# One list of the order of all instructions replaced by another: attention read and gated MLP on one core

## The chip, the cores and the metric

The kernel runs on one core of a Trainium2 chip. The metric is the device time of one execution in microseconds (us), the median of a few runs. TensorE is called PE in the profile, its weight loads PEld, VectorE DVE, ScalarE ACT, and SP is the SyncE queue from which this kernel issues all of its DMAs.

## What is computed

```
# x: B=8, H=8, S=512, D=64      state: B=8, H=8, Ns=32, D=64
scores  = scale * x @ state^T              # 512 x 32 for each (b, h)
xread   = softmax(scores)  @ state
scores2 = scale * state @ x^T              # 32 x 512
sread   = softmax(scores2) @ x
t = concat([xread, sread], axis=2)         # 8 x 8 x 544 x 64
t = t.transpose(0, 2, 1, 3).reshape(-1, 512)   # the reference reshapes these 4352 rows ...
out = ((t @ w_a) * (t @ w_b)) @ w_out      # d_model 512, d_ff 1536
```

The result is fp32. Nearly all of the work is the gated MLP: three products of some 4,350 tokens with matrices of 512 x 1536.

## The kernel before, in words

Every fp32 operand of a large product is split into a high and a low part (`_h`, `_l`), and a product is three matmuls: high by high, high by low, low by high. The names in the profile are tiles: `x_raw` and `stg` hold inputs as loaded, `wo` is a pool of 512-wide tiles that serve as scratch (loaded states, weights in the making, identity matrices), `raw` and `p_raw` hold fp32 values on their way to a split, `p_h`, `p_l` are split weights, `at_h`, `at_l` split tokens, `ab` is the PSUM of layer 1, `a_sb` its product, `g_h`, `g_l` the split gate result, `acc` the PSUM of layer 2 and `ms` the PSUM of everything small. `out<-stg` stores the result.

Tokens are taken batch by batch, d_ff in chunks; the attention of a batch comes ahead of its tokens, and the state reads (`raw<-e_dram`, `sd_h<-xn`, then the PE group `ms<-raw,sd_h`) are made in four places, the first of them about half way.

What sets the order: the code does not issue its instructions as it goes. A `Recorder` notes each operation as a unit with a running number, 0 to 4595 (2699 units on PE, 837 on DVE, 695 on ACT, 365 DMAs on SP). A unit is one to a few dozen instructions on one engine. A text `ORDER` (lines 137 to 323) lists all unit numbers, `arranged` reads it, and the end of `attn_moe` issues the units in that order:

```python
    with tc.manual_schedule():
        for i in arranged(rec.units):
            for obj, method, args, kw in rec.units[i].calls:
                getattr(obj, method)(*map(real, args), **{k: real(x) for k, x in kw.items()})
```

So every instruction has line L1105 in the profile, and each engine and the SP queue work through their own units in the order of the list. Waits between engines follow from the tiles. A DMA on SP waits until its tile is free, until its data are there, and for the eighth DMA ahead of it to have landed, since eight semaphores are used in turn; whatever stands behind it on SP waits with it.

Units that are spoken of below, with what they do:

| units | engine | what |
|---|---|---|
| 34; 107 | PE | `ms<-x_raw`, 8 matmuls; the second for the next input |
| 62, 68 | SP | loads `raw<-w_out` |
| 106 | SP | second load of `x_raw` |
| 204, 208; 997, 994 | SP | loads `wo<-wl`; `wo<-sd` (512 KB each) |
| 137, 138; 295, 296, 576 | SP | loads `wo<-xt` of states, 64 KB each |
| 18, 59, 60 | ACT, ACT, PE | a split `p_l`; `at_h<-ab`; the PE matmul that needs `at_h` |
| 61, 66, 80 | ACT, ACT, PE | `at_l<-ab`; `wo<-t`; the PE matmul that needs `at_l` |
| 205, 108, 109 | ACT, ACT, PE | `t<-wo`; `x_nat<-ms`; the transposes that need `x_nat` |
| 139, 160 | PE | `ms<-p_raw,wo`, 32 matmuls, which needs 137 and 138; then the first `acc<-wo,g_h` |
| 2649, 2651, 2653, 2656, 2667 | SP | last five loads for the first state read, 64 KB and (2667) 512 KB |
| 2668 | PE | the group `ms<-raw,sd_h` that needs them |
| 4467, 4471, 4475; 4513 | ACT | copies `stg<-acc`; a copy `a_sb<-ab` |
| 4511 | PE | the matmul `ab<-x_raw,wq`, 256 wide |

Of the kernel before, what the change touches and what calls it, by code (L numbers as in the profile page):

```python
# [142 lines left out]
73 144 120 135 192 105 136 150 145-146 209-210 200 214 201 151 2672 226 211 152-154 528 213 196 147 218 148 362 149  # L143
215 188 529 156 189 530 155 193 217 190 157 197 191 172 366 173 219 174-175 222 176 221 194 177 158 178 223 370 198
232 184 228 195 535 531 179 233 253 202 235 180 234 181 199 237 256 236 238 203 182-183 227 259-260 185 532 254 374
239 229 240-242 536 159 262 363 263 297 533 224 186 225 534 230 243 294 244 364 249 257-258 365 378 255 298 264 231
284 367 245 281 537 368 265 290 187 291 384 246-247 369 541 248 285 803 266 250 267 540 268 372 542 282 251 269 577
271 371 270 252 272 261 300 373 1004 273 287 277 288 299 274 375 275 289 301 998 283 324 376 325 302 538 276 1002
303-304 377 539 305-306 278 292 379 327 307 380 279 390 996 1022 318 386 391 319-320 393 308 392 309 314 310-311 394
312 346 381 347 286 321 280 322 385 313 543 382 387 315 388 330 767 326 546 354 1031 331 544 332 1013 348 355 383 518  # L150
349 356 333-334 357 1006 335-336 316 547 337-338 342 317 339-341 545 560 395 549 396-397 548 323 350 1005 328 343 398
351 550 329 344 358-359 562 352 551 399 353 401 804 563 402 768 400 552 360 411 553 361 414 417 403 407 404 554-555
405 1007 406 412 423 564 424-425 561 426 1008 565 415 408 420-421 413 556 1009 416 442 451 557 389 558 429 452 430 422
1014 448 453 431 427 454 428 1015 418 568 345 419 443 409 439 455 440 432 1000 445 1016 446 433-434 1017 435 578 410
# [993 lines left out]
```

## Time and profile before

| | |
|---|---|
| median of 3 runs | 669.38 us (669.19 to 669.46) |
| profiled execution | 669.68 us, of which the span of the trace is 667.8 us |
| granted TensorE clock in it | 1.0 of full speed |
| PE busy | 655.6 us (98% of the span) |
| PEld, DVE, ACT busy | 521.8, 438.1, 384.3 us |
| DMA queue | 122.71 MB, 55.4% of 16 engines |

The span is counted from the first instruction to the last; the 1.9 us between it and the execution's time lie around it. Each run is one execution on one core.

### The profile page before, as it was taken

To read this page: it belongs to the slowest core of one execution; us is meant where nothing else is said; L and a number is where in the kernel's file an instruction comes from. 1 tells how busy PE (TensorE), PEld (TensorE's weight loads), DVE (VectorE), ACT (ScalarE), POOL (GpSimd) and SP (SyncE) were. 2 spreads that over 40 slices of the span, in tenths; PEclk is the share of its full clock that TensorE was granted. 3 is DMA by queue.
4 is the path that set the end of the run, shared out by engine and by line. 5 is a ranking of instruction groups with operands and counts; after the bars stand their busy time and mean duration, and the time that the engine had idled before them with its cause. 6 is when DMAs were issued, how large, how long until landed. Compare 5 with 4: busy or idle time off the path is not lost.

```text
span 667.8 us, 10023 instructions
## 1 busy us (share of the span) xinstructions
PE 655.6 (98%) x3676; PEld 521.8 (78%) x3676; DVE 438.1 (66%) x837; ACT 384.3 (58%) x712; POOL 0.7 (0%) x6
## 2 busy tenths in 40 slices
PE   5999999999999999999999999999999999999997
PEld 1677777778888887887887887888888888888886
DVE  5889988875645567867667475846857545565433
ACT  4887763779986776866534343535556444454333
POOL 0000000000000000000000000000000000000000
PEclk9999999999999999999999999999999999999999
DMA  8878422296899759865865558756067230512002
GB/s 319 280 230 268 145 65 92 95 353 228 288 310 316 249 165 315 271 222 183 275 210 152 196 163 250 246 186 226 27 206 240 75 127 0 190 31 79 1 0 111
DMA packets 59776, 123.34 MB, mean 185 GB/s; under 512 B 9936, under 2 KB 18384, under 8 KB 59728
## 3 DMA queue, kind: packets, MB, share of 16 engines
q1 hardware_dynamic: 59728, 122.71, 55.4%
q8 instruction: 29, 0.48, 0.3%
q14 instruction: 19, 0.16, 0.1%
HBM read 85.46 MB, written 37.22 MB: 184 GB/s over the span
## 4 chain that ended last, share of the span: by engine, by line
PE 95%; DMA 3%; DVE 0%; issue 0%; SPq 0%; ACT 0%; ACTq 0%
PE ab L1105 44%; PE acc L1105 42%; PE ms L1105 9%; DMA wo<-xt 1%; DMA raw<-w_out 1%; DMA raw<-wl 1%; DVE p_raw L1105 0%; SPq L1105 0%; DVE t L1105 0%; ACT t L1105 0%; DVE stg L1105 0%; ACT a_sb L1105 0%; DVE m L1105 0%; ACTq L1105 0%
## 5 line engine op out<-in xcount | busy, mean ns | idle before, releaser
L1105 PE MATMUL acc<-wo,g_h 128*128 128x512 f32 (+1 forms) x824 | 268.9, 389 | 0.0
L1105 PEld LDWEIGHTS acc<-wo,g_h 128*128 128x128 f32 x824 | 153.7, 188 | 33.0 <-issue 1.7
L1105 PE MATMUL acc<-wo,g_l 128*128 128x512 f32 x412 | 153.9, 389 | 0.0
L1105 PE MATMUL ab<-at_l,p_h 128*128 128x512 f32 x384 | 148.8, 391 | 0.0
L1105 PE MATMUL ab<-at_h,p_h 128*128 128x512 f32 x384 | 147.0, 394 | 0.0
L1105 PE MATMUL ab<-at_h,p_l 128*128 128x512 f32 x384 | 146.9, 391 | 0.0
L1105 DVE TENSOR_TENSOR a_sb<-ab,a_sb 128x512 f32<-128x512 f32 (+1 forms) x108 | 71.2, 659 | 113.2 <-PE ab L1105 68.5
L1105 ACT COPY a_sb<-ab 128x512 f32<-128x512 f32 x120 | 67.9, 567 | 112.4 <-PE ab L1105 96.9
L1105 ACT CAST g_h<-a_sb 128x512 fp32r<-128x512 f32 (+1 forms) x108 | 64.2, 598 | 54.4 <-DVE a_sb L1105 34.5
L1105 DVE TENSOR_TENSOR g_l<-a_sb,g_h 128x512 fp32r<-128x512 f32 (+1 forms) x108 | 70.8, 657 | 32.5 <-ACT g_h L1105 25.1
L1105 PEld LDWEIGHTS acc<-wo,g_l 128*128 128x128 f32 x412 | 77.3, 188 | 16.5 <-issue 0.8
L1105 PEld LDWEIGHTS ab<-at_h,p_h 128*128 128x128 f32 x384 | 71.9, 188 | 22.8 <-issue 2.1
L1105 PEld LDWEIGHTS ab<-at_h,p_l 128*128 128x128 f32 x384 | 72.1, 188 | 17.6 <-issue 2.5
L1105 PEld LDWEIGHTS ab<-at_l,p_h 128*128 128x128 f32 x384 | 72.1, 188 | 15.6 <-issue 0.8
L1105 DVE TENSOR_TENSOR p_l<-p_raw,p_h 128x512 fp32r<-128x512 f32 x72 | 48.6, 683 | 15.0 <-ACT p_h L1105 14.8
L1105 ACT CAST p_h<-p_raw 128x512 fp32r<-128x512 f32 x72 | 43.2, 621 | 14.8 <-PE ab L1105 13.5
L1105 DVE SCALAR_TENSOR_TENSOR t<-t,t 128x512 int32<-128x512 int32 x60 | 41.1, 685 | 10.4 <-ACT t L1105 9.3
L1105 ACT ACTIVATE t<-raw 128x512 f32<-128x512 f32 x42 | 28.3, 674 | 5.4 <-issue 1.0
L1105 ACT CAST wq<-raw 64x512 fp32r<-64x512 f32 x40 | 24.6, 618 | 9.8 <-DVE raw L1105 8.3
L1105 PE MATMUL ms<-wq,sd_h 128*128 128x512 f32 x72 | 28.0, 390 | 0.0
L1105 PE MATMUL ms<-wq,sd_l 128*128 128x512 f32 x72 | 28.0, 389 | 0.0
L1105 ACT COPY sw_st<-ms 128x512 f32<-128x512 f32 x40 | 22.5, 586 | 7.0 <-PE ms L1105 6.0
(131 smaller groups left out, 600.4 us busy)
## 6 DMA issues: line engine op xcount, KB each, us to landing
p_raw<-scr SPq DMA_DIRECT2D x36, 512.0 KB, 5.1
raw<-wl SPq DMA_DIRECT2D x34, 512.0 KB, 6.0
scr<-sw_st SPq DMA_DIRECT2D x40, 256.0 KB, 5.6
out<-stg SPq DMA_DIRECT2D x33, 256.0 KB, 4.9
scr<-wo SPq DMA_DIRECT2D x32, 256.0 KB, 3.3
wo<-wl SPq DMA_DIRECT2D x10, 512.0 KB, 7.2
x_raw<-xt SPq DMA_DIRECT2D x8, 576.0 KB, 6.0
raw<-w_out SPq DMA_DIRECT2D x8, 512.0 KB, 4.8
```

The lines of the kernel that those rows point to most:

```text
L1105: getattr(obj, method)(*map(real, args), **{k: real(x) for k, x in kw.items()})
```

## The change

Only the text `ORDER` is replaced. The new list holds the same numbers, so the kernel issues the same instructions on the same engines, in another order on each engine and on SP. Its beginning, the place of the first state read and its end, as lines of the diff:

```diff
 ORDER = """
-5 1 6 10-11 19 23 121-122 34 994 3 35 2 520 36 137 4 8 7 37 576 0 48 62 9 38 68 20-21 521 39 22 25 49 40 24 50 522 26
-12 51 27 13 41 52 16-17 106 42 123 53 43 295 28 204 54 31 63 44 997 64 14 208 32 55 45 56 296 57 15 46 18 138 525 47
-58 65 74 59 75 29 70 76 69 293 523 77 60 30 107 71 61 524 66 212 526 80 216 67 108 78-79 124 81 206 109 86 125 33 110
-90 72 91 126 92 995 82-83 111 84-85 127 93 112 94-95 87 128 139 113 88 129 160 140 96 114 130 97 115 142 131 98 116
-163 102 166 169 141 527 167 99 143 100 164 205 117 132 101 118 170 220 89 161 133 103 119 134 168 162 207 104 165 171
...
-2584 2110 2116 2650 2127 2112 2128 2667 2117 2165 2651 2129 2054 2130 2748 2131 2121 2656 2143 2755 2133 2586 2120
...
-2761 2187-2188 2177-2178 2762 2226 2179 2196 2763 2668 2181 2749 2158 2750 3186 2154 2189 2677 2202 2680 2197 2674
...
-4469 4539 4467 4477 4470 4506 4475 4507-4508 4471 4509-4510 4519 4513 4511 4522 4478 4515 4525 4540-4541 4516
...
+0 5 34-35 1 6 10-11 19 23 3 2 520 36 62 4 121 521 8 7 122 37 68 9 48 38 20 39 21-22 204 25 49 40 24 50 522 26 12 51 41
+27 13 52 16 14 123 106 42 53 43 137 295 997 31 54 44 17 55 32 64 63 45 994 56 28 15 57 46 525 47 58 65 74 18 75 59 76
+523 69 60 70 77 66 29 71 107 138 61 205 208 80 108 212 216 524 293 576 81 78 540 124 79 109 67 206 526 207 220 86 125
+110 30 82 33 296 83 126 111 127 84 90-91 85 92-93 112 94-95 87 128 139 113 88 72 114 129 160 163 166 96-99 167 140 115
...
+2049-2051 2118-2119 2138 2755 2740 2744-2746 2140 2649 2656 2653 2667 2651 1935 1866 3184 2113 2116 2168 2155 2117
+2143 2578 2169 2167 2747 2120 2147 2156 2148-2149 2748 2144-2146 2756 2170 2174 2171 2760 2122 2175 2668 3166 2749
...
+4449-4452 4445-4446 4453-4454 4447-4448 4457 4459 4472-4474 4455-4456 4496 4475 4458 4497-4501 4460-4463 4502-4506
+4512 4469 4507-4511 4513 4515 4519-4520 4540-4541 4470-4471 4539 4542-4544 4548-4552 4514 4516-4518 4545-4546 4522
```

## Rows read from the trace of the kernel before

**Rows 1.** The profile's page: busy time by engine, and the chain that ended last.

```profile
PE 655.6 (98%) x3676; PEld 521.8 (78%) x3676; DVE 438.1 (66%) x837; ACT 384.3 (58%) x712; POOL 0.7 (0%) x6
...
PE 95%; DMA 3%; DVE 0%; issue 0%; SPq 0%; ACT 0%; ACTq 0%
```

**Rows 2.** Windows: length, then busy PE, PEld, DVE, ACT, POOL; clock, DMA share, GB/s.

```profile
0.00:10.00 10.00, 3.02 (x12) 0.92 (x12) 2.73 (x6) 3.43 (x5) 0.70 (x6) 1.00 0.78 272
10.00:20.00 10.00, 8.41 (x65) 3.55 (x65) 8.89 (x20) 6.94 (x17) 0.00 (x0) 1.00 0.98 353
20.00:30.00 10.00, 9.78 (x72) 6.14 (x72) 8.65 (x20) 8.98 (x18) 0.00 (x0) 1.00 0.97 341
30.00:90.00 60.00, 60.00 (x348) 44.51 (x347) 55.31 (x103) 44.99 (x83) 0.00 (x0) 1.00 0.59 190
90.00:640.00 550.00, 550.00 (x3056) 446.36 (x3055) 352.18 (x669) 311.52 (x574) 0.00 (x0) 1.00 0.55 183
640.00:668.00 28.00, 24.35 (x129) 20.34 (x127) 10.30 (x23) 8.46 (x18) 0.00 (x0) 1.00 0.18 66
```

**Rows 3.** The chain that ended last, 0 to 30 us: start, length, what.

```profile
10.52 7.08 DMA raw<-w_out
...
19.43 8.41 DMA wo<-xt
```

**Rows 4.** Timeline of PE, 0 to 35 us and 58 to 110 us.

```profile
4.41 1.94 PE L1105 MATMUL ms<-x_raw 128*32 128x512 f32 x8 [4.41 <-DMA x_raw<-xt]
...
21.37 1.07 PE L1105 MATMUL ms<-x_raw 128*32 128x512 f32 x8
...
26.68 1.07 PE L1105 MATMUL ms<-p_raw,wo 64*32 64x256 f32 x16
27.97 1.07 PE L1105 MATMUL ms<-p_raw,wo 64*32 64x256 f32 x16 [0.22 <-DMA wo<-xt]
28.97 0.50 PE L1105 MATMUL acc<-wo,g_h 128*128 128x512 f32 x1
...
80.67 1.20 PE L1105 MATMUL ms<-p_raw,wo 64*32 64x256 f32 x32
```

**Rows 5.** Timeline of the SP queue, 0 to 24 us: start and length of the issue.

```profile
16.12 0.33 SPq L1105 DMA_DIRECT2D x_raw<-xt  x1
...
18.74 2.25 SPq L1105 DMA_DIRECT2D wo<-xt  x2
```

**Rows 6.** DMA issues, 0 to 30 us: count, KB each, median us to landing.

```profile
wo<-xt SPq DMA_DIRECT2D x5, 64.0 KB, 7.6
```

**Rows 7.** Timeline of ACT, 16 to 33 us.

```profile
18.79 0.66 ACT L1105 CAST p_l<-acc 128x256 fp32r<-128x256 f32 x2
...
19.96 0.59 ACT L1105 CAST at_h<-ab 128x512 fp32r<-128x512 f32 x1
...
30.77 0.68 ACT L1105 ACTIVATE t<-wo 128x512 f32<-128x512 f32 x1
```

**Rows 8.** Timeline of the end, all engines, 653 to 668 us.

```profile
653.42 1.57 ACT L1105 COPY stg<-acc 128x512 f32<-128x512 f32 x3 [0.99 <-PE acc L1105]
...
654.86 0.39 PE L1105 MATMUL acc<-wo,g_h 128*128 128x512 f32 x1
655.06 0.37 ACT L1105 COPY a_sb<-ab 128x256 f32<-128x256 f32 x1
...
655.48 0.39 PE L1105 MATMUL ab<-x_raw,wq 128*128 128x256 f32 x1 [0.23 <-ACT a_sb L1105]
...
661.51 0.30 PEld L1105 LDWEIGHTS acc<-wo,g_l 128*128 128x128 f32 x2 [0.16 <-DVE g_l L1105]
```

**Rows 9.** First state read: SP timeline, PE timeline, DMA issues 330 to 348 us.

```profile
336.33 1.46 SPq L1105 DMA_DIRECT2D raw<-e_dram  x2
...
347.29 0.65 PE L1105 MATMUL ms<-sd_h,raw 128*32 128x64 f32 x32
...
raw<-e_dram SPq DMA_DIRECT2D x7, 64.0 KB, 5.3
```

More of the change, by code (lines that the diff above doesn't have):

```diff
@@ new lines @@
+901 1252 1204 942 946-949 927 1215 928 1193-1194 1216 1205 924 1207 1206 920 1253-1254 925 1327 1208 943 926 929 1225
+1195-1196 1221 923 954 931 950 932 963 1222 951 1249 1237 964-965 952 991 1250 1209 870 1320 1210 960 955-956 1319
+1218 982 966 1226 972 1321 961 1255 973 1239 1217 1223 1322 1101 644 1219 1211 1103 1102 967-968 1212 969-971
+1323-1324 1220 1104 974-975 1325 992 962 1227 957 1228 976-977 958 978 1224 1328 1238 993 959 979 1229 1326 980 1240
+1336 1256 953 988-989 1230 1105 1329 1111-1112 1241 1330 990 1231 1331 1257 1113-1116 1233 981 1232 1106-1108 1234
@@ new lines @@
+1109-1110 983-984 1332-1334 985 1335 986 1127 1354 987 1356 1130 1345 1117 871 1128-1129 1242 1355 1357 1118 1155 1124
+1370 1337 1358 1371 1131 1133 1359 1235 1134-1135 1119 1372 1360 1243 1338-1342 1125 1156 1120 1126 1139 1347
+1140-1141 1152 1236 1132 1142 1158-1159 1361 1343-1344 1402 1244 1153 1346 1373 1364 1160 1136-1138 1287 1258 1475
+1348 1362 1260 1145 1143 1259 1363 1349-1351 1261 2679 1374 1144 1262 1157 1284 1121 1378 1146 1263 1379 1365 1375
+1264 1288 1122 1394 1285 1352 1268 1123 1353 1380 1289 1381 1265-1267 1366 1269 1367 1270-1271 1368 1376 1272 1369
@@ new lines @@
+1286 1154 1149-1150 1274 1147-1148 1377 1281-1282 1403 1395 1273 1408 1290 1382 1275 1404 1151 1276-1277 1384 1405
+1383 1283 1309 1312 1291 1385 1315 1292 1278 1414 1293 1316 1294 1477 1295 1386 1390 1296-1298 1397 1299 1302 1387
+1398 1391 1300 1313 2285 1314 1441 1409 2060 1301 1406 1396 1310 1392 1279-1280 1306-1308 1435 1303-1304 1415
+1410-1411 1305 1311 1438-1440 1442-1443 1436 1417 1478 1416 1418 1317 1546 1479 1407 2294 1388 1466 1419-1422 1467
+1668 1444-1445 1400 2287 1423-1425 1431 1426-1428 1480 1429-1430 2286 1447-1449 1437 1468 1432 1450-1452 1459 1412
@@ new lines @@
+1446 2288-2289 1453-1456 2290-2291 2720 1481 1463 1457 1464 1469 1607 1389 1458 1393 1465 1482 1433 1460 1401
+1483-1484 1399 1434 1470 1461 1488-1489 1485 2292 1462 1498 1486 1472-1474 1507 1487 2293 1413 2295 2303 2296 2712
+2321 1494 2297 1501 2323 1490-1491 2298 1471 2299-2300 1510-1513 1547 1492-1493 1495 1499 1504-1506 1500 1514 1496
+2301-2302 2312 1497 1548 1476 1515 1534-1535 1508-1509 1516-1521 1608 1526-1527 1502-1503 1536 1530-1532 1522 2322
+2324 1549 2304 1538 1523 1539 1551 2305 1528 1552 2325 1550 1557 1553-1554 2306 1672 1529 1537 1567-1568 1533 1669
@@ new lines @@
+1609 1555 1558 1610 1540 2307 1556 1541 2327 1559 1563 1560 1570 2308 1561-1562 1579-1580 1564 1524 1573 2309 1576
+1571 1581 2326 2313 1582 2314 1574 2328 1583 2315 1585-1586 2310 1587 2316 1577 2337-2338 2340 2339 1569 1611 1525
+2317 1572 1595 1584 2318 1588 2311 1589 2331 1591 2406 1590 2329 1544 1741 2319 1592 1596 2330 1612-1615 1578
+1604-1605 2320 1616 1618 1565 1673-1674 2415 2341 1566 1617 1624 1675 1598-1600 1631 1597 1619 2407 1628 2333-2334
+1575 1620-1623 1640 1625 2408 2332 1593 2342 2409 1641 2410 2669 1594 1629 1642 1632-1633 1643 1601 1644-1645 2061
@@ new lines @@
+1602-1603 1634 2411-2413 1652 1659 1626 2062 2417 1646-1648 2414 2063 1676 1606 1637-1638 1649-1651 2416 2424 2080
+2733 2067 1627 1653 1802 1677-1679 2343 2418 1680 1635-1636 1662 2064 1681-1682 2419 1639 1683-1684 2420-2421 1665
+1654 2422 1630 2065 2423 1656-1657 1660 2078-2079 2335 2068 1689 1658 1685-1686 2336 2081 2069 1687-1688 2083 2344
+1663 1661 1666-1667 1702-1703 1690 2433 2426 1864 2066 2442 2082 1705 1693 2070 1696 1711-1715 2673 1742 2425 2427
+1706-1709 2428 2071 1691 1542 2444 1664 1699-1701 1655 2086 1744 2443 2458 1692 1697 2445 1710 1717 1545 1694 1704
@@ new lines @@
+2446 1803 2447 1733 1746 2429-2430 1698 1725 2435 1743 1695 2431 1734-1736 1716 1726 2448 2432 1727-1728 2449 2527
+1747 1721 2434 2461 2450 1729-1731 1718 1748 1543 1722-1723 2436 1745 2072 1740 2459 1752-1753 1724 1754-1755
+1749-1751 2452 1805 1758 1719 1756 1762 2437 1732 1757 1763 2438-2439 1804 1759 1739 1863 2529 2073-2074 2440 2460
+1867 1774-1778 2528 2441 1806 2530 1764 1720 2536 1780-1781 1779 1786 1765 1768 1771-1773 1769-1770 1766 1796
+1782-1784 1790-1792 1785 2531-2533 2075 1799-1800 1807-1811 1760-1761 2451 2453 2463 2462 1812 1819 1787 1767 1793
@@ new lines @@
+1788 1794 1789 1823 1813 2534 1824 1814-1815 2535 1816 2545 1835-1836 1817-1818 1936 1820 2734 1868 1870 1837
+2454-2455 1838 1869 2537 1797 1839 1841-1844 1840 2538 1847 2539 2456 2076 1845-1846 1795 1826 2457 1872 1871 2077
+1873 1997 1798 1801 1832-1833 1829 2464 1848 1878-1879 1830 1827-1828 1831 1821 1874-1877 1822 2084 2540-2543 1849
+2544 1884 1880-1882 1670 1937 1939 1671 2085 2465 1737 2554 1834 2546 1860 2721 1938 1940 2547 1825 2087 2565 1854
+1851 1855 2563-2564 2548 1852 2566 2579 1900 1861 1901 1883 1885 1902 1856 1891-1892 1862 1897 1903-1904 1893 1905
@@ new lines @@
+2094 2580 2732 2088 1850 1912 2089-2091 1898-1899 2567-2568 2581 1928 2549 2670 1906 1857-1859 1894-1896 1924 1920
+1853 1888-1889 1941 1907 2718 1942 1886-1887 1921 1908 2550 1909 1890 1916-1918 1910-1911 1929 1922 1943 1913
+1944-1945 2551 1946 1914 1925 1953 1930 2556 1919 2569 1915 1926-1927 1923 1947 2652 1969-1973 1998 1738 1948-1950
+2552 1957 1999 2570 1951-1952 2000 2555 2557-2558 1954 2559 1960 2735 2560-2561 1958 2736 1934 1974 1981 2562
+1975-1976 2553 2648 2658 2657 1963-1964 1977 1959 1978-1979 1931 2752-2753 2092 1961-1962 1988 1955 1980 1966 2737
@@ new lines @@
+1982 1967 1983 1965 2001 2741 2738 2665 2163 2650 1968 1994 2664 2002 1991 2003 1865 2008 2004 1985-1987 1995 2009
+2005 2010 2006 1989 2582 2666 2007 1932 2661 2011-2013 2571 1956 2014-2015 2030-2033 1996 1990 2021 2739 2036 2572
+2095 2097 2027-2028 2037-2039 2034 2040 2093 2029 2654 2055 2583 1984 2096 2098 2224 2659 2041 2056 2035 2042
+1992-1993 2024-2026 2018-2019 2573 2164 2016 3169 2022 2099 2574 2100 2742 2101 2057 2124 2020 2102 2754 2043 2575
+2584 2103 2576 2104 2663 2743 2105-2106 2660 2125 2585 2577 2655 2107 2044 2108 2662 2046-2048 2115 2052 2109-2110
@@ new lines @@
+2345 2690 2181-2182 2197-2200 2190-2192 2201 2694 2700 2697 2202-2204 2212 2208 2158 2758 2213 2205-2206 2228 2162
+2759 2207 2193-2195 2229 2214 2685 2209 2183 2217 2709 2696 2692 2218 2245 2701 2586 2707 2693 2230 2683 2686 2684
+2346-2347 2688-2689 2231 2235 2246-2247 2236 2210 2232 2219-2220 2233-2234 2221 2241 2222 2237-2240 2242-2243 2223
+2257 2254 2251 2255 2211 2263-2264 2252 2258-2261 2265-2268 2248-2249 2262 2269-2271 2466 3187 2348 2706 2703 2691
+2695 2705 2349 2587 3221 2708 2698 2764 2256 3188-3190 2282 3193 2283 2273-2275 2284 2366-2367 2253 2279 2244 2702
@@ new lines @@
+2250 2276-2278 2369 2350 2280 2351 2281 3191 2352 2765-2767 3194 2467 2272 2356-2359 2372-2374 2360-2361 2353-2355
+2362-2364 2469 2365 3206 2468 2375 3192 3207 2376-2377 2368 2394 2378-2379 2395 3208 2403-2405 2380-2384 2396
+2385-2389 2710 2390-2391 2470-2477 2483 3195 3151 3256 2370-2371 2397 2392 2719 3161 2713 2768 3257 2588 2716 2722
+2590 3204-3205 3209 3196 2398 2589 2591 2399 2478-2482 2484 2490 2499-2500 2496-2498 2524 2723 3142 3152 2393
+2400-2402 2485-2486 2505 2731 2729 2501 3143 2506-2507 3220 3154 2837 2502-2503 2491 2504 2511 2508 3212 2509
@@ new lines @@
+2493-2494 2510 2592-2593 3163 2487-2489 2515 3277 2512 3213 2726 3197-3200 2160 3157 2730 3214-3215 3164 2513 2769
+2728 2725 3172 2770 2594-2597 2604 2771 2727 3201 3222 3202 2525 2772 2516 3158 3160 3145 2492 2526 2518-2520 3173
+3203 2724 2611-2613 2617-2618 2495 3210 2898 3211 3144 3261 2598-2601 2620 2602-2603 2517 2608 2514 2605 2521-2523
+2614 2621 2609 2615-2616 2642-2643 2622 2626-2629 2623-2624 2610 2630 2625 2631 2639 2606 3159 3156 3155 3264 3150
+3280 2644 2632-2633 2607 2636 2634 2838-2839 2637 2773-2774 2619 3149 2161 2779-2780 3146 3263 2781-2784 2775-2778
@@ new lines @@
+2785 3170 2786 3223 3216 2801 2645 2795 2646 2640 2647 2798 2807 2641 2808-2811 3148 3265 3217 3153 3147 2796 2638
+2789-2791 2802-2806 2635 2813 3218 2812 2799-2800 3224 3278 3226 2814 2829 2817 2842-2843 2818-2819 2792 2899 2840
+2820 2841 2959 2830-2831 3167 3227 3225 3229 2900 2848 2793-2794 2821-2822 2849 2823-2824 3240 2834 3283 3259 3258
+2844-2847 2797 2850-2853 2825-2827 2787 2815 2788 2858-2860 2886 2854 3162 3228 2855-2856 2828 2816 3281 2861 3349
+3165 2832 3171 2870-2881 2887 2862 3232 2901 3233 2864 3234-3235 2857 3219 3230-3231 2863 2865-2866 2902 2867-2869
@@ new lines @@
+2895 3020 2882 2903 2883 2904-2907 2909-2914 2884 3260 3275 3174 2889 3168 2960 2892 2962 2893 2890 2908 2915 3175
+2891 3236 3284 3176 2888 2919-2920 2922 2931 2916 2937-2938 2894 2923-2924 2896 2950 2932-2933 3237-3238 2961 2963
+2885 3183 2934 2921 2917 3241 3245 3239 3246 3286 2935 2939-2940 2897 3287 3081 2936 2951 2943 2941 2947 3247 2948
+2925 2942 3266 2926 2928-2929 3262 2964 2927 2944 2965 3267 3302 3242-3243 2918 2966 2930 2967-2968 3268 2969 2976
+2945 3021 3274 3269-3270 2953 2970-2975 2949 2992-2993 3023 3271-3272 2954 2994 3181 2946 3273 2995 2159 3180
@@ new lines @@
+2996-2997 2952 2983 2955 2986-2987 3004 2988 3244 3022 2977 3014-3015 2998-3001 3025 3002 2980 3024 3082 3003 3005
+3016 2956-2958 2978 2989 3026-3029 3031 2990-2991 3017 3304 3248 3084 3249 2979 3030 3276 3037 2981 2984 3279 3053
+3288 3282 3018 3032 3006 3033-3034 3019 3035 2982 3047 3285 3008 3289 3036 3050-3052 3078 3038 3054-3058 2985
+3011-3012 3007 3013 3059-3060 3009 3355 3308 3404 3486 3083 3048-3049 3410 3085 3061 3178 3294 3290-3291 3062 3065
+3063-3064 3303 3305 3445 3039 3306 3309 3079 3010 3041 3080 3066 3179 3250 3293 3310 3075 3044 3086 3311 3451 3092
@@ new lines @@
+3087-3089 3042-3043 3090-3091 3093-3094 3312 3069 3076 3045 3350 3046 3040 3077 3072 3095 2833 3096 3307 3297 3296
+3351-3352 3313 3842 3537 3353-3354 3357 3182 3108 3098 3292 3097 3073 3300 3074 3070-3071 3099 3109 3067 3114 3110
+3115-3117 3295 3068 3487 3111 3488 3118 3112 3177 3105 3119 3126 3298 3100 3106-3107 3133 3489 3299 3102-3103 3113
+3301 3139-3140 3356 3406 3134 3490 3358 3848 3120-3124 3314 3125 3315 3359 3104 3127 3405 3101 3130-3131 3316 3128
+3317 3889 3318 3360 3407 3319 3322 3136 3323 3538 3411 3408 3412-3413 3324 3320 3141 3346 3325-3328 3129 3321 3330
@@ new lines @@
+3540 3331 3446 3414 3135 3598 3137 3329 3409 3138 3447 3340-3342 3332-3333 3415 3453 3334 3388 3343-3344 3132
+3337-3339 3361-3363 3345 3364-3366 3335-3336 3369 3367-3368 3370 3377 3371-3376 3347 3378 3348 3396 3380 3389 3379
+3384 3416 3381 3417 3424 3448 3425 3382 3385-3386 3383 3426 3449 3427 3418-3419 3387 3420 3450 3421-3422 3452 3423
+3539 3428 3432 3429-3431 3392 3454 3433 3455 3397-3398 3435 3390 3393-3394 3456-3457 3391 3439 3465 3458-3459
+3466-3467 3460-3462 3434 3436-3438 3468-3470 3463-3464 3395 3473 3471-3472 3474 3476 3844 3843 3402 3442 3895 1933
@@ new lines @@
+3985 3944 3541 3659 3401 3400 3440 3443-3444 3483-3484 3441 3480 3485 3491 3475 3845 3492-3493 3497-3501 3494 3477
+3846 3478 3847 3479 3495-3496 3503 3510 3481 3502 3482 3849 3504 3511-3512 3399 3505 3251-3252 3513-3515 3519
+3516-3518 3520 3525 3521-3524 3507-3508 3599 3509 3542-3545 3506 3526-3527 3529-3530 3546 3531 3558-3559 3532 3601
+3561 3548 3547 3549 3564 3550 3554 3551-3553 3570-3573 3562 3565-3566 3592-3593 3574 3560 3586 3555 3600 3602
+3576-3577 3528 3563 3575 3578 3582 3579-3581 3587 3603 3589 3583 3720 3533-3534 3590 3609 3535 3604 3536 3605-3607
@@ new lines @@
+3782 3784 3688 3893-3894 3705 3678 3897 3706 3682 3679 3707 3717-3718 4388 3898 3945 3719 3711-3712 3714 3750 3708
+3715-3716 3747-3748 3709 3751-3752 3946 3783 3947 3731 3778 3948 3737 3951 3899 3779 3732-3736 3710 3749 3741 3738
+3900 3949 3785 3952 3742-3743 3769 3753-3759 3775 3765 3760-3761 3770 3762 4429 3739 3763-3764 3786 3766 3787-3792
+3771 3780 3793-3796 3811 3797 3953-3954 3713 3744-3746 3772-3774 3805-3806 3740 3798 3807 3814 3799 3815-3817
+3820-3822 3818-3819 3767 3833 3776 3823-3825 3802-3804 4027 4029 4028 4030 3768 3834 3777 3826 3854-3859 3835 3800
@@ new lines @@
+3830 3808-3810 3836-3838 3801 3860 3827 3862-3864 3861 3870 3812-3813 3865-3867 3883 3831 3987 3828-3829 3901 3868
+3871 3869 3873 3872 3874 3986 3988 2836 4435 4077-4078 3403 3902 3992 3832 3903-3907 3839-3840 3875 3841 3876 3880
+3908 3917 3989-3990 4138 4484 3909-3915 3884 3916 4080 3886-3888 3885 3932 3881 3918 3920 3882 3877-3879 3924-3928
+3933 3929-3930 3936 3931 3979 3937 3956-3957 3934 3958-3960 3919 3955 3993 4384 3994 4383 3921-3923 3940 4385 3995
+3964-3965 3961 3996 3962-3963 3972 3966-3970 3973 3935 3974 3971 3997-3999 3975 4000-4002 3976 4003 3938 3977
@@ new lines @@
+4121 4143-4147 4123 4162 4124 4134 4165 4149-4150 4148 4097 4155 4436 4151-4153 4166 4154 4127 4163 4200 4202 4156
+4128 4157 4171 4167 4193 4177-4178 4437 4125 4179-4180 4159 4194 4170 4160 4158 4181 4172-4173 4438 4485 4182
+4174-4176 4195-4198 4229 4226 4230 3942 4260 3943 4490 3941 4528 4231 4227 4261 4183 4204-4205 4201 4203 4321 4184
+4486-4487 4262 4185 4210 4206-4209 4211 4263 4491 4212-4215 4257 4216 4228 4232-4235 4164 4190-4192 4223-4225 4254
+4258 4217 4238 4264 4161 4187-4189 4220-4222 4248-4249 4218 4186 4250 4259 4219 4439 4239-4241 4236-4237 4244
@@ new lines @@
+4281-4283 4242-4243 4488 4322 4265-4266 4245 4267-4269 4246 4270-4273 4277 4440 4324 4255-4256 4290-4291 4323 4293
+4274 4294 4247 4275 4292 4318 4251 4276 4319 4287 4309-4310 4295-4298 4305 4325 4492 4278 4299-4304 4326-4327 4306
+4252 4279 4253 4284 4328 4285 4332-4334 4286 4335-4336 4329-4330 4311 4342-4343 4331 4489 4337 4320 4288 4351-4352
+4280 4338-4339 4353 4530 4289 4354-4355 4360 4356 4361 4312 4362 4357-4359 4493 4529 4307-4308 4344 4370-4371
+4313-4314 4345 4372 4315-4317 4348 4340-4341 4379 4363 4349-4350 4376 4364-4366 4394-4401 4410 4377-4378 4346
@@ L323 @@
+4561 4527 4567-4568 4575 4562 4576-4577 4585-4587 4574 4581 4588 4582-4583 4594 4569 4584 4593 4570-4571 4578-4580
+4589-4592 4595
 """
```

225 lines of the change are left out of this document (48 added, 177 removed).

## Prediction

> **What bounds the kernel now.** Read the page first: PE is busy for 655.6 us, 98% of the span, and the chain that ended last is PE for 95% and DMA for 3% [rows 1]. The instructions are the same in both lists, so PE's work is too; a new order can only change the time in which PE has none. The windows say where that is. From 30 to 640 us PE is busy in every microsecond; it loses 8.8 us in the first 30 us (6.98, 1.59, 0.22) and 3.65 us in the last 28, most of them after its last matmul [rows 2]. So there are two places to look at, and one to fear: the middle, which has nothing to gain and anything to lose.
>
> The chain of the first 30 us shows what the start hangs on: DMA, not an engine. A load `raw<-w_out` lands at 10.52 + 7.08 = 17.60 us, and a 64 KB load `wo<-xt` (unit 138) at 19.43 + 8.41 = 27.84; the matmuls of 27.97 follow on that [rows 3]. In PE's timeline the group of 32 `ms<-p_raw,wo` (unit 139) is cut in two there: 16 at 26.68, 16 at 27.97, together 29.04 - 26.68 = 2.36 us, and the next matmul starts 2.29 after the group began. A later group of the same 32 takes 1.20, at 80.67. So the late load costs 1.16 us [rows 4].
>
> **The start, part by part.** The first matmuls stay. Unit 34 waits for the first `x_raw` load, at the head of SP in both lists, and takes 1.94 us where unit 107, the same 8 matmuls, takes 1.07 [rows 4]. The Trainium skill (TensorE: Matmul & The Clock Gate, Part 1) has a level of 1.2 GHz for an array that was idle and 2.4 GHz for one that is busy; the two durations look like that, though the clock column of the windows shows 1.00 throughout [rows 2, 4], and it changes nothing in the sum, since the new list doesn't make the early work denser.
>
> SP: in the new list a `w_out` load (62) goes ahead of the second pair of `stg` loads, and 68 right behind the pair; the `wo<-sd` loads 994 and 997 and the spare state loads 576 and 296 go back, and 138 goes ahead of 208, 296 and 576. The state load 138 was issued last of a pair from 18.74 on [rows 5], once `x_raw` could go at 16.12, when its tile came free. That load (106) keeps its time, so 138 can't be issued before about 18.4. When it lands is a matter of bytes: the DMA share was 0.98 and 0.97, at 353 and 341 GB/s [rows 2], and a load of only 64 KB takes 7.6 us there [rows 6]: it lands when what stands ahead of it has landed. Ahead of 138 stand now 640 KB fewer (512 for 208, twice 64) and nothing more. At 341 GB/s this is 1.9 us: it lands at 27.84 - 1.9 = 25.9 at the latest. By its issue and its own queue it could be 23.4: some 1.8 MB from 106 to 138, behind what is in flight until about 18.0. Either is early enough for a group that begins at 26.7 or later and needs 138 for its second half. The Trainium skill (DMA: Bandwidth & Descriptors, Specifications) gives about 358 GB/s as the HBM limit of a core. The windows' 353 agrees with that, and it speaks against hope for more from an earlier issue; by it the 640 KB are 1.8 us, and the sum stays.
>
> What is late next: ACT and DVE. `w_out` lands some 3.6 us earlier (about 14.0), so the wait that ended at 17.60 goes [rows 3], but ACT's order changes too. The split 18 (one of two `p_l` that take 0.66 together) stands ahead of 59, which ran from 19.96; with 0.25 us for it, `at_h` for unit 60 is there at 19.96 + 0.25 + 0.59 = 20.8 [rows 7], and 107, two matmuls behind 60, starts at 21.5 where it was 21.37 [rows 4]. `wo<-t` (66) stands ahead of 61: unit 80 at 22.55, 0.2 later. Unit 205 stands ahead of 108 (0.68, some 0.6 from start to start [rows 7]): 109 at 23.65, 0.25 later. From there to 139 both lists have the same matmuls, back to back: 139 at 26.68 + 0.26 = 26.94. It needs no wait any more, and 160 follows at 26.94 + (2.29 - 1.16) = 28.07, where it was 28.97 [rows 4]. **Start: 0.9 us earlier.** Bounds: 1.16 if ACT's slips are absorbed, 0 if another 0.9 us of slips comes on top of the 0.26 (ACT is 8.98 of 10 us busy from 20 to 30 us, DVE 8.65 [rows 2]). I take 0.87, for I followed the units one by one with the durations they have in the trace.
>
> **The end.** In the old list the copy of `a_sb` (4513) stands behind three copies of `stg`, 1.57 us that begin at 653.42. It starts at 655.06, and PE waits 0.23 for it: the 256-wide matmul (4511) starts at 655.48, 0.62 after the one before it, at 654.86 [rows 8], where 0.23 is usual between two of these matmuls. In the new list 4511 stands ahead of 4513, so it can't wait for it, and 4513 ahead of 4471. **Gain 0.39.** The other wait, for `g_l` at 661.51 (0.16, about 0.2 with what follows [rows 8]), may shrink: between the last `ab` matmul and the first that needs this `g_l` lie 2.8 us of PE's work now and 2.2 before. I take half, 0.1; bounds 0 and 0.2, and for both -0.1 to 0.6. The stores after the last matmul are the same.
>
> **The middle.** 610 us with no PE wait in any window [rows 2], and nearly every line of the list differs in it. I compared, for each matmul, the last ACT, DVE or DMA unit that it needs, by the PE work that lies between: the closest are 0.15 to 0.2 us away in both lists, and as many (28) under 0.3 us in each. So I cost the middle at a loss of 0.1; bounds +0.5 (the small waits of before, two of about 0.28 us, gone) and, for a loss, the rivals. Cover is thinnest at two places. From 30 to 90 us DVE is busy for 55.31 of 60 us [rows 2]; 4.69 us are left, of which a start that is 0.9 earlier uses up to 0.9. And at the first state read: its last loads were issued from 336.33 to about 337.1 and, at 5.3 us to landing, are there at 342.4 to 342.8, 4.5 us before the group at 347.29 [rows 9]. In the new list the group (2668) comes 3.4 us of PE work earlier, and the last five loads stand later, behind a load that waits for a matmul some 11.6 us before the group. Six issues of about 0.45 us each, then 5.3: 3.6 us left at best; with the eighth-before rule some 1.7. Still covered.
>
> **The sum.** 0.87 + 0.39 + 0.1 - 0.1 = 1.26 us off the profiled execution's 669.68: 668.42. The median of the runs is 0.30 below that execution, and the same work is taken off it: 669.38 - 1.26 = 668.12, say 668.1. What a measurement of this kernel can tell from no change is about 0.2%, 1.34 us: faster is below 668.04, slower above 670.72. So the forecast lies next to the lower bound.
>
> **Rivals.**
> *Everything comes off*: ACT's slips are absorbed (1.16), both end waits go (0.6) and the middle gains its small waits (up to 0.5): 2.0 to 2.3, at 667.1 to 667.4. For it: the middle of a list drawn up anew may shed what 0.28 us waits it has. Against: ACT's slips follow from the order of three pairs, and ACT is nearly full there. 0.2.
> *The lead is eaten*: DVE at 92% in 30 to 90 us holds PE back until the 0.87 are gone; the end's gain is left: 669.38 - 0.4 = 669.0. For it: the busy share; against: PE never waited there, and DVE's idle 4.69 us are five times the lead [rows 2]. 0.17.
> *Nothing happens*: 138 is as late as before, since the queue is no shorter for it, or another load takes its place (106 landed just ahead of 107): 669.3. 640 KB less speak against it. 0.06.
> *The other side*: the five loads of the first state read go out when the units around them in the list do, about 4.1 us of PE work before the group, at some 338.9 us, and not at 334. Five issues of 0.43 and 5.3 to landing make 346.3, where the group could start at 343.0: a stall of some 3.3 us, and 668.1 + 3.3 = 671.4. It decides from a stall of 2.6 us on. For it: the list puts them there. Against: SP runs ahead of the list's neighbours as soon as its own waits are met, and none of the five waits for anything at 338.9. 0.12, with lesser places of this kind.
>
> **How the numbers follow.** The forecast has 0.45, its own range 667.7 to 668.6; about 0.17 of it lies under 668.04. Faster: 0.17 + 0.2 = 0.37. Within 0.2%: 0.28 + 0.17 + 0.06 = 0.51. Slower: 0.12. The range has to hold the forecast, the eaten lead and nothing (0.68) and some of the two outer cases: 667.2 to 670.1.
>
> **What would show it.** 160 (the first `acc<-wo,g_h`) at 28.0 to 28.2 with no cut in the group of 32 before it; 138 landed between 23.4 and 25.9; 107 at 21.4 to 21.6; windows of 10.00 for PE from 30 to 640; the group `ms<-raw,sd_h` without a DMA wait; no PE wait for `a_sb` some 10 us before the last matmul. It is wrong if the first 30 us gain nothing, if DVE is the releaser of PE between 30 and 90 us, or if any DMA appears as a releaser of PE after 30 us.

## The result and the profile after

The kernel with the new list takes 674.06 us (median of 6 runs, 672.99 to 674.71) where the old one takes 669.38: 1.0069 times as long, 95% interval 1.0057 to 1.0082. The forecast was 668.1, in a range of 667.2 to 670.1. The profiled execution took 674.09 us, with a span of 672.1.

The windows are those of [rows 2] (columns as there):

```profile
10.00:20.00 10.00, 8.61 (x62) 3.15 (x63) 9.35 (x20) 6.10 (x15) 0.00 (x0) 1.00 0.94 350
20.00:30.00 10.00, 9.96 (x78) 6.47 (x77) 8.04 (x18) 8.78 (x19) 0.00 (x0) 1.00 0.92 313
30.00:90.00 60.00, 59.51 (x345) 43.75 (x344) 55.31 (x105) 44.56 (x83) 0.00 (x0) 1.00 0.49 163
90.00:640.00 550.00, 547.62 (x3038) 442.64 (x3037) 348.64 (x663) 308.36 (x571) 0.00 (x0) 1.00 0.56 186
```

The middle, which had 610 us without a PE wait, now has 0.49 + 2.38 us of them. The view of waits says for what (engine and tile, released by, us in all, times, longest):

```profile
PE ms L1093 <- DMA x_raw<-xt: 4.4, 1, 4.4
PE ab L1093 <- ACT a_sb L1093: 3.4, 5, 1.2
PE ab L1093 <- DMA stg<-xt: 1.7, 1, 1.7
```

Five waits of the `ab` matmuls for an ACT copy `a_sb<-ab`, where the old kernel had one of 0.23 [rows 8]. No DMA holds PE after the start. In the timeline four of the five look alike, here with the copy ahead of each:

```profile
481.75 0.37 ACT L1093 COPY a_sb<-ab 128x256 f32<-128x256 f32 x1
...
482.17 0.39 PE L1093 MATMUL ab<-x_raw,wq 128*128 128x256 f32 x1 [1.24 <-ACT a_sb L1093]
...
564.35 0.37 ACT L1093 COPY a_sb<-ab 128x256 f32<-128x256 f32 x1 [0.81 <-DVE g_l L1093]
...
564.77 0.39 PE L1093 MATMUL ab<-x_raw,wq 128*128 128x256 f32 x1 [0.52 <-ACT a_sb L1093]
...
576.63 0.37 ACT L1093 COPY a_sb<-ab 128x256 f32<-128x256 f32 x1 [0.28 <-PE ab L1093]
...
577.05 0.39 PE L1093 MATMUL ab<-x_raw,wq 128*128 128x256 f32 x1 [0.46 <-ACT a_sb L1093]
...
662.51 0.86 ACT L1093 COPY a_sb<-ab 128x512 f32<-128x512 f32 x2 [0.48 <-PE ab L1093]
...
663.42 0.39 PE L1093 MATMUL ab<-x_raw,sw_st 128*128 128x256 f32 x1 [0.65 <-ACT a_sb L1093]
```

(The line of 662.51 holds two copies, the second of them 256 wide.) Each time a 256-wide matmul into `ab` starts 0.05 us after a 256-wide copy out of `ab` has ended. The code that both come from is the layer 1 of the unit that holds the state tokens, whose 256 tokens stand twice in one tile, high parts in columns 0 to 255, low parts behind:

```python
                    nc.tensor.matmul(ps, lhsT=wh, rhs=x.rearrange("p a n -> p (a n)"), start=(k == 0), stop=(k == 3),
                                     skip_group_check=True)
                    nc.tensor.matmul(ps[:, :self.n], lhsT=wlo, rhs=x[:, 0], start=False, stop=(k == 3), skip_group_check=True)
...
            nc.scalar.copy(out=t[:, n:], in_=both[1][:, n:])
```

The last matmul of a tile writes columns 0 to 255 and the copy reads 256 to 511. They share no data, so a list may put the copy ahead of that matmul. But they share the tile, and where the copy stands first, the matmul waits for it. The trace also tells what holds it: of the 24 matmuls that finish a tile of this layer 1, these four and no others wait for a semaphore, number 102, which ACT's copy raises when it is done. So the wait is one that the program asks for, and the order in the list settles whether it does. The new list does this in four places (3331 ahead of 3329, 3871 of 3869, 3973 of 3971, 4557 of 4555). The old list does it in two: 3918 ahead of 3916, where the copy had ended 0.97 us before, and 4513 ahead of 4511, the wait of [rows 8].

Where the 4.3 us of span went is read by comparing the two traces where PE has the same work behind it. In this table a line is a point in PE's work (the sum of the usual times of the matmuls ahead), and a number is how much later than in the old kernel PE is there. The values depend on the usual times that are put in, and are good to about 0.2; the steps that are read from them below are larger, or are marked as small places:

```
PE work    after    e1     e2     e3     e4     e5     e6     e7     e8
  10       0.86   1.11   0.55   0.56  -0.39   0.81   0.32   0.15  -0.18
  20      -0.26  -0.07   0.03   0.39  -0.60  -0.34  -0.85  -0.99  -0.61
  52      -0.26  -0.07   0.03   0.39  -0.60  -0.34  -0.85  -0.97  -0.61
  60       0.52   0.71   0.01   0.42  -0.59  -0.11  -0.09  -0.99  -0.40
 150       0.92   1.12   0.02   0.43  -0.60   0.18   0.29  -0.98  -0.10
 455       1.27   1.16   0.03   0.38  -0.62   0.26   0.53  -0.93   0.00
 500       2.80   1.13   2.05   0.41  -0.58   0.29   0.53  -0.92   0.01
 550       3.62   1.15   2.05   0.41  -0.58   0.32   1.34  -0.92   0.04
 600       4.27   1.07   3.05   0.42  -0.60   0.24   1.99  -0.93  -0.04
 634       4.19   0.99   3.05   0.42  -0.60   0.16   1.91  -0.93  -0.12
 638       3.69   0.49   3.05   0.42  -1.10  -0.34   1.40  -1.44  -0.63
 644       4.39   0.30   3.51   0.41  -1.16  -0.54   2.10  -1.46  -0.82
```

The column "after": 0.26 won in the start; 0.78 lost at 52 to 60 (the fifth wait, 0.49, and what follows); 0.4 by 150 and 0.35 more by 455, in small places; then 1.5, 0.8 and 0.7 at the first three of the four pairs; 0.5 won where 4511 stands ahead of 4513, as forecast; and at the fourth pair 0.9 lost at once, 0.7 by the end of the table. The other columns are the experiments.

### The profile page after: what moved, and what is told of

Same layout as the page of the kernel before. It is cut to its first block, busy times and chain, and to the rows that moved or that the text cites. A ratio compares the mean times of both kernels' runs of the same rounds, so it can differ in the third digit from the quotient of the medians.

```text
span 672.1 us, 10047 instructions
## 1 busy us (share of the span) xinstructions
PE 657.1 (98%) x3676; PEld 520.9 (78%) x3676; DVE 438.1 (65%) x837; ACT 382.7 (57%) x712; POOL 0.7 (0%) x6
## 4 chain that ended last, share of the span: by engine, by line
PE 93%; DVE 3%; ACT 2%; DMA 1%; issue 1%; SPq 0%; DVEq 0%; ACTq 0%
PE ab L1093 43%; PE acc L1093 40%; PE ms L1093 10%; DMA wo<-wl 1%; DVE t L1093 1%; DVE g_l L1093 0%; SPq L1093 0%; ACT a_sb L1093 0%; DVE p_l L1093 0%; DVE xst L1093 0%; ACT t L1093 0%; DVE a_sb L1093 0%; DVE s_p L1093 0%; ACT g_h L1093 0%; DVE m L1093 0%
## 5 line engine op out<-in xcount | busy, mean ns | idle before, releaser
L1093 PE MATMUL acc<-wo,g_h 128*128 128x512 f32 (+1 forms) x824 | 265.9, 389 | 0.0
L1093 PE MATMUL acc<-wo,g_l 128*128 128x512 f32 (+1 forms) x412 | 153.6, 388 | 0.0
L1093 PE MATMUL ab<-at_l,p_h 128*128 128x512 f32 x384 | 147.3, 390 | 0.0
L1093 PEld LDWEIGHTS acc<-wo,g_l 128*128 128x128 f32 x412 | 77.2, 188 | 16.2 <-issue 0.8
```

## The experiments

Every kernel computes the whole result; only `ORDER` differs. Ratios are to the old kernel in the same set of runs.

| run | us, median | ratio to before | 95% interval |
|---|---|---|---|
| e1, new list, four pairs turned | 669.59 | 0.9994 | 0.9985 to 1.0002 |
| e2, old list, four pairs as in the new | 673.63 | 1.0055 | 1.0042 to 1.0069 |
| e3, old list, state load 138 earlier | 669.67 | 0.9993 | 0.9985 to 1.0002 |
| e4, e3 and 4511 ahead of 4513 | 669.25 | 0.9986 | 0.9977 to 0.9994 |
| e5, e1 and two copies of `ab` earlier | 669.31 | 0.9990 | 0.9981 to 0.9999 |
| e6, new list, one pair turned | 672.00 | 1.0038 | 1.0024 to 1.0051 |
| e7, e4 and load 204 earlier | 668.32 | 0.9979 | 0.9969 to 0.9988 |
| e8, e5 and ACT's start order | 669.36 | 0.9995 | 0.9986 to 1.0004 |

**e1: the four matmuls ahead of the copies, in the new list.**

```diff
-... 3540 3331 3446 3414 3135 3598 3137 3329 3409 ...
+... 3540 3329 3331 3446 3414 3135 3598 3137 3409 ...
-... 3868 3871 3869 3873 ...
+... 3868-3869 3871 3873 ...
-... 3970 3973 3935 3974 3971 3997 ...
+... 3970-3971 3973 3935 3974 3997 ...
-... 4554 4557-4558 4555 4479 ...
+... 4554-4555 4557-4558 4479 ...
```

> The changed list with four matmuls moved up, each ahead of the a_sb copy that stands just before it in the list (3329 ahead of 3331, 3869 of 3871, 3971 of 3973, 4555 of 4557); the copy reads one half of an ab tile and the matmul writes the other half. Theory A (a matmul that follows a copy of its tile in the list waits for that copy, though they share no data): the PE waits at 482, 565, 577 and 663 us go, which are 1.5, 0.8, 0.7 and 0.9 us: 674.06 - 3.9 = 670.2, and no PE wait for a_sb after 100 us. Rival B (ACT is simply late in the changed list and holds the ab banks): the waits move a few matmuls on, less than 1.5 us come back, 672.6 or more. Rival C (the loss lies elsewhere, in many small places): 673.5 or more.

669.59, the same as the old kernel: 4.5 us of the 4.7 are gone by the medians (4.1 by the table, of which the four places make 3.7 to 3.9), and with them every wait for `a_sb` after 100 us; what is left in the view of waits is the one near 68 us:

```profile
PE ab L1093 <- ACT a_sb L1093: 0.5, 1, 0.5
```

At the same copies the order is now the other one: ACT waits for PE, and not PE for ACT, and none of the 24 matmuls waits for a semaphore any more. The second of the four (the line of 562.12 holds two matmuls, the second of them 3869):

```profile
562.12 0.51 PE L1093 MATMUL ab<-x_raw,wq 128*128 128x512 f32 x2
...
562.66 0.37 ACT L1093 COPY a_sb<-ab 128x256 f32<-128x256 f32 x1 [0.88 <-PE ab L1093]
```

Theory A stands; B and C fall.

**e2: the copies ahead of the matmuls, in the old list.**

```diff
-... 3141 3329 3413 3337-3338 3361 3129 3362 3344 3363 3331 3345 ...
+... 3141 3331 3329 3413 3337-3338 3361 3129 3362 3344 3363 3345 ...
-... 3837 3869 3861 3838 3870 3832 3841 3877 3871-3872 ...
+... 3837 3871 3869 3861 3838 3870 3832 3841 3877 3872 ...
-... 3931 3971 3997 4385 3938 3973 4020 ...
+... 3931 3973 3971 3997 4385 3938 4020 ...
-... 4558 4555 4526 4557 4527 ...
+... 4558 4557 4555 4526-4527 ...
```

> The old list with the same four pairs put as in the changed list: the four a_sb copies moved up, each to just ahead of the matmul into the other half of its tile. Theory A: the old list now waits in these places too, each time for what is left of the copy when PE gets there, 0.5 to 1 us a place: 669.4 + 2 to 3.5 = 671.4 to 672.9, with four PE waits for a_sb that the old list did not have. Rival B (the waits come from ACT's backlog in the changed list, not from the order of the pair): the old list has none, 669.2 to 669.8.

673.63, 0.7 above the top of what was expected, of which 0.4 is that the old kernel itself took 669.76 in this set of runs. The old list, with nothing else moved, loses 3.5 us by the table and 3.9 by the medians, where the new one loses 4.7. Its waits in the view of waits:

```profile
PE ab L1105 <- ACT a_sb L1105: 3.2, 4, 1.7
```

and in the timeline

```profile
481.63 0.38 PE L1105 MATMUL ab<-x_raw,wq 128*128 128x256 f32 x1 [1.75 <-ACT a_sb L1105]
...
576.23 0.39 PE L1105 MATMUL ab<-x_raw,wq 128*128 128x256 f32 x1 [0.72 <-ACT a_sb L1105]
...
662.52 0.38 PE L1105 MATMUL ab<-x_raw,sw_st 128*128 128x256 f32 x1 [0.46 <-ACT a_sb L1105]
```

These are three of the four places; the fourth wait of the view is the old one near 655 us. The pair 3871 and 3869 cost nothing here: the matmul now waits for ACT's semaphore like the others, but the copy was done 1.24 us before it starts at 562.77. So the order of a pair makes the wait possible, and ACT's lateness sets its length, from 0 to 1.75 us.

**e6: one of the four pairs.** The first of the four edits of e1, alone.

> The changed list with only the first of the four pairs repaired (matmul 3329 ahead of the copy 3331, near 482 us). Theory A: this place alone is worth 1.5 us, and the four add up: 674.06 - 1.5 = 672.6, with three PE waits for a_sb left after 100 us. Rival (the waits are not independent, a PE that comes earlier waits longer at the next): 673.5 or more.

672.0, 2.1 below the new list and 0.6 below what was expected; in the two profiles the 0.6 lies in the start (-0.85 against -0.26 at 20). In the table its column is flat from 455 to 500, where "after" steps by 1.5, and takes the other steps at their full size (0.8, 0.65 and 0.7). The waits are independent and add up.

**e3 and e4: the start's load, and the pair at the end, in the old list.**

```diff
-... 64 14 208 32 55 45 56 296 57 15 46 18 138 525 ...
+... 64 14 138 208 32 55 45 56 296 57 15 46 18 525 ...
```

and in e4 besides

```diff
-... 4519 4513 4511 4522 ...
+... 4519 4511 4513 4522 ...
```

> The old list with one move: the 64 KB state load 138 goes two places ahead on SP, in front of the 512 KB load 208 and of 296. By the prediction's first step the load lands at about 25.4 instead of 27.84, the group of 32 ms<-p_raw,wo is not cut, the first acc<-wo,g_h starts at 27.8 to 27.9 instead of 28.97: 669.38 - 1.1 = 668.3. Rival (something else is as late as the load, ACT's g_h at 28.06 or the split p_h): 0.3 us or less, 669.1.

> As the run with the state load moved, and at the end the 256-wide matmul 4511 ahead of the copy 4513. By theory A the PE wait near 655 us (0.39 from start to start) goes too: 669.38 - 1.1 - 0.4 = 667.9, faster than both kernels. Rival (the time comes back before the end, at the next wait for g_l): as the run with the state load alone.

e3 gave 0.1 us by the medians, 0.5 by the ratio (its interval reaches from a loss of 0.1 to a gain of 1.0), and not 1.1: the rival, and behind the late `g_h` that it names stands DVE, as shown below. e4 took 669.25 and not 667.9; its last step (638 in the table) is the 0.5 us of the pair 4511 and 4513. What held the group of 32 once its load was there is seen in e4's timeline of DVE and PE:

```profile
24.24 0.43 DVE L1105 TENSOR_SCALAR t<-wo 128x512 int32<-128x512 uint32 x1 [1.36 <-DMA wo<-wl]
24.58 1.28 DVE L1105 TENSOR_REDUCE m<-ms 128x16 f32<-128x512 f32 x2
25.78 1.28 DVE L1105 TENSOR_TENSOR s_p<-ms,m 128x512 f32<-128x512 f32 x2
...
26.56 1.67 PE L1105 MATMUL ms<-p_raw,wo 64*32 64x256 f32 x32 [0.24 <-issue]
28.36 0.50 PE L1105 MATMUL acc<-wo,g_h 128*128 128x512 f32 x1
```

DVE stands in line behind another load (204, `wo<-wl`), and its two `s_p<-ms,m`, which free `ms`, end at 27.06, half a microsecond after the group began; the group takes 1.67 us and not 1.20, and the next matmul waits for `g_h`, which comes through the same DVE.

**e7: that load earlier too.**

```diff
-... 16-17 106 42 123 53 43 295 28 204 54 ...
+... 16-17 204 106 42 123 53 43 295 28 54 ...
```

> The old list with the state load 138 and the end's pair as in the run with both, and the 512 KB load 204 moved ahead of 106 and 295 on SP. Theory: in the old list DVE waits 0.7 to 1.4 us for 204 (t<-wo at about 24 us), so its two s_p<-ms, which free the ms bank for the group of 32, and ACT's g_h behind them come late, which is why the state load alone gave 0.1 us of 1.1. With 204 earlier the group takes 1.13 us and the first acc<-wo,g_h starts at 27.6 to 28.0: 669.25 - 0.6 = 668.6. Rival (the x_raw load 106 is now late, 512 KB behind): unit 107 waits for it, 669.3 or more.

668.32, faster than both kernels (0.9979, 0.9969 to 0.9988). From e4 to e7 that is 0.5 us by the ratios, whose intervals overlap, and 0.6 in the profiles by the start of the first `acc<-wo,g_h` (28.36 and 27.75). DVE no longer waits for a DMA there, and the group is whole:

```profile
23.06 0.43 DVE L1105 TENSOR_SCALAR t<-wo 128x512 int32<-128x512 uint32 x1
...
26.61 1.20 PE L1105 MATMUL ms<-p_raw,wo 64*32 64x256 f32 x32
...
27.75 0.50 PE L1105 MATMUL acc<-wo,g_h 128*128 128x512 f32 x1
```

**e5 and e8: the rest of the new list.** In e5, on top of e1,

```diff
-... 547-548 1014 342 395 ...
+... 547-548 342 1014 395 ...
-... 1027-1028 1090 724 739 ...
+... 1027-1028 724 1090 739 ...
```

and in e8, on top of e5,

```diff
-... 74 18 75 59 76 523 69 60 70 77 66 29 71 107 138 61 205 208 80 ... 540 124 79 ...
+... 74-75 59 18 76 523 69 60 70 77 29 71 107 138 61 66 208 80 ... 540 124 205 79 ...
```

> The changed list with the four pairs repaired, and two copies of ab moved up by one place on their engine: on ACT the a_sb copy 342 ahead of a t<-wo (near 68 us), on DVE the a_sb product 724 ahead of a t<-wo (near 125 us). These are the two other places where PE loses time by the trace of the changed kernel, 0.65 and 0.3 us. Theory: order on ACT and DVE alone costs them, 669.6 - 0.95 = 668.6, with no PE wait after 30 us. Rival (the engines are full there, the wait moves on): 669.4 or more.

> As the run with six places repaired, and ACT's order near 20 us put back: 18 behind 59, 66 behind 61, 205 behind the two x_nat copies. By the prediction's second step these three pairs cost 0.2 to 0.4 us of the start: 668.6 - 0.3 = 668.3, faster than both kernels. Rival (the start is bound by the time at which TensorE's clock rises, not by ACT): 668.6.

e5 has no PE wait after 30 us in the view, as expected, but gained 0.3 us by the medians and not 0.95. By the table 0.55 of it came back between 52 and 60; near 110 the 0.3 only moved to a place before 150. e8 gained nothing (669.36): its group of 32 took 1.66 us, as in e4, although load 204 landed at 17.76, as early as in the new list. The timelines of DVE and PE show why:

```profile
22.11 0.69 DVE L1093 TENSOR_TENSOR wo<-t,wo 128x512 fp32r<-128x512 f32 x1 [0.29 <-ACT wo L1093]
...
23.89 0.69 DVE L1093 SCALAR_TENSOR_TENSOR wq<-t,t 128x512 int32<-128x512 int32 x1 [0.57 <-ACT t L1093]
...
25.70 1.28 DVE L1093 TENSOR_TENSOR s_p<-ms,m 128x512 f32<-128x512 f32 x2
...
26.48 1.66 PE L1093 MATMUL ms<-p_raw,wo 64*32 64x256 f32 x32
28.28 0.97 PE L1093 MATMUL acc<-wo,g_h 128*128 128x512 f32 x3
```

With 66 and 205 back behind 61 and 108, DVE waits 0.29 and 0.57 us for them, and its two `s_p<-ms,m` end at 26.98, again half a microsecond after the group began. In e6, which has the new list's order here, DVE has neither wait and the first `acc<-wo,g_h` starts at 28.01. So these pairs are not a plain cost, as the prediction had them: they also bring DVE on time. What they cost or gain in all stays open, since the clock moved the start by more from run to run (below).

## Why the prediction was wrong

**What bounds the kernel**: right. PE's work is the same, the middle had nothing to gain and "anything to lose", and it lost it.

**The middle**: here the prediction failed, in the step "I compared, for each matmul, the last ACT, DVE or DMA unit that it needs". A matmul also waits for units whose data it doesn't need: for a copy out of its tile that stands ahead of it in the list. Comparing by data gave 28 close pairs in each list and a loss of 0.1; the pairs that mattered had no data between them. The four of them cost 1.5, 0.8, 0.7 and 0.7 to 0.9 us (3.7 to 3.9), and e1 and e2 show it in both directions. In the sum the middle stands with a loss of 0.1; by the table it lost some 4.4 from 20 to 634, 3.0 of them at the three pairs that lie there. The evidence was at hand: the wait of 0.23 for `a_sb` in [rows 8] is one of these pairs. The prediction used it for its own place (4511 ahead of 4513 "can't wait for it", 0.39 forecast, 0.5 measured) and did not ask where else the new list makes such a pair.

**The start**: the load came early as said, but its size hung on a term that was put at nothing. The load 138, issued at 18.61, landed at 24.93, within 23.4 to 25.9, and the group of 32 took 1.20 us without a cut. (It came 2.9 us earlier, and not the 1.9 that 341 GB/s would give. The 353 GB/s of the windows is no ceiling here: the trace before, cut into slices of 0.75 us, has up to 433 in its first 30 us.) But the first `acc<-wo,g_h` came 0.33 earlier than before (0.26 by the table), and not 0.87:

```profile
16.25 1.94 PE L1093 MATMUL ms<-stg 128*32 128x512 f32 x8
...
22.18 1.07 PE L1093 MATMUL ms<-x_raw 128*32 128x512 f32 x8
...
27.50 1.20 PE L1093 MATMUL ms<-p_raw,wo 64*32 64x256 f32 x32
28.64 0.98 PE L1093 MATMUL acc<-wo,g_h 128*128 128x512 f32 x3
```

The 8 matmuls `ms<-stg` took 1.94 us; in the profile before, the same 8 took 1.15. They still ran at the slower of the two rates in which the 8 matmuls of [rows 4] come (1.94 and 1.07). e6 has the same start, and there they took 1.17, and all behind them is 0.63 earlier:

```profile
16.41 1.17 PE L1093 MATMUL ms<-stg 128*32 128x512 f32 x8
...
21.55 1.07 PE L1093 MATMUL ms<-x_raw 128*32 128x512 f32 x8
...
26.86 1.20 PE L1093 MATMUL ms<-p_raw,wo 64*32 64x256 f32 x32
28.01 0.96 PE L1093 MATMUL acc<-wo,g_h 128*128 128x512 f32 x3
```

21.55, 26.86 and 28.01 stand beside the forecast's 21.5, 26.94 and 28.07, and the start won 0.96 (0.85 by the table). The old list does not pay for slow matmuls in this way. In e2, which has its start, they took 1.93 us, and the first `acc<-wo,g_h` still starts where it did in the kernel before (28.97):

```profile
16.25 1.93 PE L1105 MATMUL ms<-stg 128*32 128x512 f32 x8
...
27.17 1.89 PE L1105 MATMUL ms<-p_raw,wo 64*32 64x256 f32 x32
28.99 0.50 PE L1105 MATMUL acc<-wo,g_h 128*128 128x512 f32 x1
```

There the group waited for load 138 (landed at 27.85) in any case. So the new start is worth 0.96 where the 8 matmuls are fast in both lists (before and e6) and 0.35 where they are slow in both (e2 and the new list). Of the two rates the prediction said that "it changes nothing in the sum"; here they changed it by 0.6, and that the forecast's times came true in e6 is in part the luck of one execution. One more thing was mis-said: the 1.16 us were not the late load's alone. In e3 and e4 that load was early and 0.5 came back; the other half needs load 204, which the new list also moves ahead (landed at 17.53, before at 23.90) and which the prediction passed over.

**The end**: the pair gave 0.5 (0.39 forecast), and the fourth pair took it back eight microseconds later. The `g_l` term (0.1) is lost in that.

**The rivals**: the state reads were in time; the group `ms<-raw,sd_h` waited for no DMA, so the one rival that ended on this side was the wrong one. "The lead is eaten" in 30 to 90 us was right as to the place: at 68.52 PE waits 0.49 for a copy that ACT reaches late, after 3.34 us in which it stood behind DVE:

```profile
66.67 0.69 ACT L1093 ACTIVATE e<-ms,m 128x512 f32<-128x512 f32 x1 [3.34 <-DVE s_p L1093]
...
67.89 0.58 ACT L1093 COPY a_sb<-ab 128x512 f32<-128x512 f32 x1
...
68.52 0.50 PE L1093 MATMUL ab<-at_h,p_h 128*128 128x512 f32 x1 [0.49 <-ACT a_sb L1093]
```

It was counted as a case of no change; with 0.78 us it alone took more than the start's 0.26.

## What to carry to other kernels

When an order of instructions is drawn up anew, compare waits by tile, not by data: list every pair in which an instruction of one engine touches a tile ahead of another engine's write to it, whether or not the columns meet, and ask of each pair that the new order turns round how late the first engine is there. A wait in the trace between two instructions that share no data is the sign that such pairs exist; look for all of its kind before pricing the rest at nothing. Shown is this for matmuls and copies of the PSUM tile `ab`; for turned pairs in other tiles it was not tried, but after 30 us the view of waits has none of PE in the new list besides the five for `a_sb`. And a load that is late for a matmul may be one of two: before crediting it with the whole wait, follow the other inputs of that matmul back to their loads.

## What the runs showed that was not expected

The moment at which TensorE's matmuls begin to take half the time is not set by the list. The 8 `ms<-stg`, which start at 16.2 to 16.8 us in all ten traces, took 1.15, 1.93, 1.33, 1.07 and 1.06 us in the five with the old list's start (before, e2, e3, e4, e7) and 1.94, 1.84, 1.38, 1.17 and 1.06 in the five with the new list's (after, e1, e5, e6, e8), though up to there each five have the same order on PE. That is up to 0.9 us from one execution to the next, as much as the whole of the start's forecast, and it blurs every comparison of starts here by single profiles. The clock column of the windows shows 1.00 in all of these stretches, but the record of the granted clock in the traces begins only later, each time with 1.00 (the level of 2.4 GHz): at 16.76 us before, 16.68 in e6, 18.04 in e2, 18.16 with the new list, and between 15.83 and 18.16 in all ten. The later it begins, the longer the 8 matmuls took, but for differences under 0.1 us. For the time ahead of it nothing is recorded, so there the durations tell the rate and the column doesn't; they are near those of the other level, 1.2 GHz. PE was busy without a pause before the rise in the kernel before and in the new one. The Trainium skill (TensorE: Matmul & The Clock Gate, Part 1) says that the point of the rise differs from run to run of the same kernel, since the hardware's look at the activity does not begin with the kernel; the ten traces agree that it differs, and the reason no run here shows.

The group of 32 `ms<-p_raw,wo` is two streams of 16 that run beside each other on PE: 1.20 us where both can start together, 1.66 or 1.67 where the second starts some 0.6 us late (e3, e4, e8), 2.36 where the two run one after the other, with 0.2 of waiting between them [rows 4].
